# Engine programs in a block with a closing barrier, or straight in the main body: a decode kernel on one core

## The chip, the cores and the metric

The kernel runs on one core of a Trainium2 chip. Its traces show five engines with instruction streams of their own, side by side: PE (matmul, busy for 63% of the span of the kernel before), DVE (vector, 64%), ACT (scalar, 14%), POOL (GpSimd, 5%) and SP (sync, which here issues every transfer in the trace's list of DMA issues, from the 4096 KB loads to the 4 KB store). The metric is the device time of one execution in microseconds (us).

The **span** is the length of the trace, from the first to the last instruction of the kernel's own program. The **time** is what counts; it is longer than the span. Their difference is called the **remainder** below. Every timed run lists both, the span to 0.1 us, so a mean of several runs gives the remainder to about 0.05 us. No trace shows where the timed execution begins: a constant part of the remainder, the same for all kernels here, may lie before the span. "The end of the timed execution" below is counted as if it began with the span; differences between kernels do not depend on that, absolute sizes do.

## The reference, cut to what matters

```python
def reference(A_x, A_k_cache, A_v_cache, A_wq, A_wo, B_x, B_W_gate, B_W_up, B_W_down, gate_w):
    ...                                               # the helpers are cut
    x = A_x
    g = _sigmoid((x * gate_w).sum(-1, keepdims=True))
    a = _A_ref(x, A_k_cache, A_v_cache, A_wq, A_wo)   # one query, window of 4096 keys, 32 heads on 8 KV heads
    b = _B_ref(x, B_W_gate, B_W_up, B_W_down)         # gated feed-forward part
    return g * a + (1 - g) * b                        # 4 x 1 x 512, bf16
```

It reads 81 MB of caches and weights and writes 4 KB.

## The kernel before

Each engine has a function that emits its program. The functions are first run without emission, which numbers the semaphore events, and then with it, inside a block:

```python
def bass_gated_mix__...(nc, A_x, ..., out):
    ...
        R = _alloc(nc, ctx)
        progs = _program(nc, plan, R, aps)
        for _, prog in progs:
            prog(None)
        for name in plan.unit:
            plan.sems[name] = ctx.enter_context(nc.semaphore(name))
        plan.emit, plan.n = True, {}
        with nc.Block() as block:
            for name, prog in progs:
                getattr(block, name)(prog)
```

What the block makes of it, as the built program shows: the main body holds the start barrier of all engines (which is there without the block too) and, for each engine, a branch to that engine's own body. Each body ends in a branch to a common closing body. There each engine drains, reports to POOL (the gathering), and waits until POOL releases them all.

The last useful work is the store of the output. SP issues it and waits for it; its wait rides on SP's branch out.

```python
    def sync(e):
        ...
        load(("OUT",), "d_out", out.rearrange("b o d -> (b o) d"), osum[:, :], waits=[("OSUM", 0), ("OSUM", 1)])
        E.wait([("OUT",)])

    def gpsimd(e):        # only the constants; POOL's program is done at 12 us
        ...
        for g in range(8):
            v = R["fold"][:, g % 4, :, :]
            aff(v, v, [[1, 4], [-1, 64]], -64 * g, ne, 1.0, ("FOLD", g), mult=4)
```

## Time and profile before

| | before |
|---|---|
| time, median of 3 runs (range) | 197.35 us (197.25 to 197.66) |
| span of the profiled run, its time | 195.3 us, 197.06 us |
| DMA | 81.01 MB read, 415 GB/s over the span |
| busiest engine | DVE, 64% |

The page of the kernel before: the span, the busy time of each engine (in us, as a share of the span, and its number of instructions), and a row of its table of forty equal slices of the span. A digit of this row is the busy share of the 16 DMA engines in tenths, and 9 means 90% or more.

```profile
span 195.3 us, 1747 instructions
...
PE 122.6 (63%) x723; PEld 51.1 (26%) x723; DVE 124.4 (64%) x153; ACT 27.5 (14%) x34; POOL 9.5 (5%) x25
...
DMA  6999999999999999999999999999999999998991
```

The DMA engines are busy for 90% or more of all but three slices, and no other engine is near that over the span: loads bound the kernel, and what a change that leaves the loads alone can still win lies before the first load and after the last one. So the two ends matter. The start, in the timeline of the kernel before (start in us, duration, engine, line, operation; in brackets the engine's idle time before it and what ended it):

```profile
0.80 1.28 ACT L598 ACT_TABLE_LOAD   x1 [0.80 <-PEq L645]
0.80 0.20 POOL L300 MEMSET ones<- 128x128 f32 x1 [0.29 <-POOLq L645]
0.80 0.39 SPq L257 DMA_DIRECT2D slots<-in_A_wq_dram  x1
...
1.35 1.98 DVE L487 MEMSET qblk<- 128x2304 uint32 x1 [1.35 <-PEq L645]
```

Line 645 is where the start barrier is made. SP issues the first load at 0.80 us. The end, in the same timeline:

```profile
193.16 0.37 ACT L624 ACTIVATE osum<-bank 4x256 bf16<-4x256 f32 x1 [8.03 <-PE bank L321]
193.19 0.42 DVE L578 CAST osum<-bank 4x256 bf16<-4x256 f32 x1 [4.29 <-PE bank L321]
193.70 0.27 SPq L257 DMA_DIRECT2D out_dram<-osum  x1
```

The timeline ends with the issue of the store at 193.70 us. The branches, drains and semaphore instructions that follow are not counted as work, but asking for the line of the block (98) shows them (count, duration in ns, then the start of the first and of the last in us; the letter q marks the engine's sequencer):

```profile
L98 POOLq EVENT_SEMAPHORE  x2: 17/17/17, 195.2 to 195.2; - x2
L98 POOLq DRAIN  x1: 497/497/497, 11.6 to 11.6; - x1
L98 PEldq DRAIN  x1: 410/410/410, 192.8 to 192.8; - x1
...
L98 SPq COMPARE_BRANCH  x1: 33/33/33, 195.0 to 195.0; - x1
L98 SPq DRAIN  x1: 7/7/7, 195.1 to 195.1; - x1
L98 SPq EVENT_SEMAPHORE  x1: 17/17/17, 195.3 to 195.3; - x1
...
L98 PEldq EVENT_SEMAPHORE  x1: 51/51/51, 195.3 to 195.3; - x1
```

The unrounded records give the order: the output landed at 194.942 us, SP's waiting branch was recorded at 194.958, SP's drain at 195.122, POOL's two instructions (gathering and release) at 195.154 and 195.232, and PE woke last, from 195.286 to 195.337. From the landing to the end of the span it is 0.395 us. Note POOL: its program was done and drained at 12 us, and it then stood in the closing barrier until 195.25.

### The profile page before, as it was taken

Reading aid. Unit: us, or ns where it says so; the run is one execution under the profiler, and the core shown is the slowest. Engines: PE = TensorE matmul, PEld = TensorE weight load, DVE = VectorE, ACT = ScalarE, POOL = GpSimd, SP = SyncE. Lnnn points to the kernel's source line nnn. Section 1 sums busy time; section 2 is a strip of 40 time slices with the busy share of each in tenths; the row PEclk is TensorE's granted clock in tenths of the full one; section 3 lists DMA queues with packets and bytes.
Section 4 is the critical chain, followed back from the end, with each engine's and each line's share of the span. In section 5 each row is a group of like instructions: output and inputs, shape, how many; then the busy total and the mean of one; then the engine's idle time right before and its main releaser. Section 6 shows DMA issues by size and latency. Waiting matters only on the chain.

```text
span 195.3 us, 1747 instructions
## 1 busy us (share of the span) xinstructions
PE 122.6 (63%) x723; PEld 51.1 (26%) x723; DVE 124.4 (64%) x153; ACT 27.5 (14%) x34; POOL 9.5 (5%) x25
## 2 busy tenths in 40 slices
PE   0209267573974797389338646865599338754975
PEld 0004122121421242133114312421133112322562
DVE  6103688999489829981998199819971997280010
ACT  2213100040031004001300130014001400420100
POOL 7830000000000000000000000000000000000000
PEclk9999859997899579969999978998769996995799
DMA  6999999999999999999999999999999999998991
GB/s 221 429 424 436 429 429 443 429 426 436 429 443 443 431 436 433 429 436 436 436 436 429 419 436 429 436 429 429 429 429 426 429 388 426 475 429 379 418 406 70
DMA packets 4046, 81.10 MB, mean 415 GB/s; under 512 B 576, under 2 KB 840, under 8 KB 1096
## 3 DMA queue, kind: packets, MB, share of 16 engines
q1 hardware_dynamic: 4040, 81.01, 97.1%
q8 instruction: 5, 0.08, 0.2%
q14 instruction: 1, 0.01, 0.0%
HBM read 81.01 MB, written 0.00 MB: 415 GB/s over the span
## 4 chain that ended last, share of the span: by engine, by line
DMA 53%; DVE 30%; PE 9%; issue 5%; SPq 1%; ACT 0%
DMA slots<-in_A_k_cache_dram 37%; DVE kt L492 21%; DMA slots<-in_A_wo_dram 9%; PE bank L321 8%; DMA gwT<-in_gate_w_dram 6%; DVE sc L528 5%; DVE qblk L518 1%; PE bank L325 1%; SPq L257 1%; DVE pT L543 1%; DVE rd L532 1%; DVE negmax L538 0%; ACT gwB L601 0%; DVE osum L578 0%; DVE mx L528 0%
## 5 line engine op out<-in xcount | busy, mean ns | idle before, releaser
L321 PE MATMUL bank<-kt,qblk 128*128 128x512 bf16 x256 | 72.6, 434 | 30.9 <-DVE kt L492 30.8
L492 DVE STREAM_TRANSPOSE kt<-slots 128x2048 f32<-128x2048 f32 x32 | 73.7, 2305 | 25.1 <-DMA slots<-in_A_k_cache_dram 25.1
L321 PEld LDWEIGHTS bank<-kt,qblk 128*128 128x128 bf16 x256 | 24.8, 106 | 73.3 <-DVE kt L492 40.1
L321 PE MATMUL bank<-slots,pT 128*64 128x512 bf16 x256 | 33.1, 417 | 4.8 <-DMA slots<-in_A_v_cache_dram 4.8
L528 DVE CUSTOM_DVE_ANT_0 sc<-bank,maskf 128x512 bf16<-128x512 f32 x32 | 21.1, 661 | 6.6 <-PE bank L321 6.6
L620 ACT ACTIVATE pe<-sc,negmax 128x2048 bf16<-128x2048 bf16 x8 | 16.0, 2002 | 58.1 <-DVE negmax L538 58.1
L321 PEld LDWEIGHTS bank<-slots,pT 128*64 128x64 bf16 x256 | 15.4, 121 | 23.1 <-issue 13.6
L543 DVE STREAM_TRANSPOSE pT<-pe 128x2048 bf16<-128x2048 bf16 x8 | 18.5, 2312 | 2.2 <-ACT pe L620 2.2
L605 ACT ACTIVATE osb<-bank 128x512 bf16<-128x512 f32 x8 | 4.8, 597 | 84.2 <-PE bank L321 84.2
L321 PE MATMUL bank<-rd,grpb 128*128 128x32 bf16 x8 | 1.5, 192 | 18.9 <-DVE rd L532 18.9
L556 DVE TENSOR_TENSOR oq<-bank,recip 64x128 bf16<-64x128 f32 x2 | 0.9, 434 | 12.3 <-PE bank L321 12.2
L321 PEld LDWEIGHTS bank<-rd,grpb 128*128 128x128 bf16 x8 | 0.8, 97 | 22.4 <-DVE rd L532 22.4
L496 DVE COPY xT<-bank 128x16 bf16<-128x16 bf16 x1 | 0.2, 166 | 8.4 <-PE bank L325 8.4
L321 PE MATMUL bank<-slots,xT 128*4 128x512 bf16 (+1 forms) x64 | 5.3, 490 | 0.0
L518 DVE TENSOR_SCALAR qblk<-bank 32x64 uint32<-32x64 uint32 x16 | 2.9, 215 | 2.9 <-PE bank L325 2.9
L321 PE MATMUL bank<-slots,oq 128*4 128x256 bf16 x64 | 4.0, 272 | 1.2 <-DVE oq L556 1.1
L321 PE MATMUL bank<-maskr,maskl 128*128 128x512 bf16 x1 | 0.6, 606 | 5.9 <-POOL maskr L297 5.9
L325 PE MATMUL bank<-identb,xsb 4*128 4x4 bf16 x4 | 0.3, 166 | 6.1 <-DMA xsb<-in_A_x_dram 6.1
L297 POOL TENSOR_SCALAR_AFFINE_SELECT fold<-fold 128x256 bf16<-128x256 bf16 x8 | 3.3, 417 | 1.1
L321 PEld LDWEIGHTS bank<-slots,oq 128*4 128x4 bf16 x64 | 2.6, 84 | 2.5 <-issue 1.3
L578 DVE CAST osum<-bank 4x256 bf16<-4x256 f32 x1 | 0.4, 418 | 4.3 <-PE bank L321 4.3
L487 DVE MEMSET qblk<- 128x2304 uint32 x1 | 2.0, 1978 | 1.4 <-PEq L645 1.4
(59 smaller groups left out, 41.4 us busy)
## 6 DMA issues: line engine op xcount, KB each, us to landing
slots<-in_A_k_cache_dram SPq DMA_DIRECT2D x8, 4096.0 KB, 25.0
slots<-in_A_v_cache_dram SPq DMA_DIRECT2D x8, 4096.0 KB, 30.0
slots<-in_A_wq_dram SPq DMA_DIRECT2D x1, 4096.0 KB, 12.5
slots<-in_A_wo_dram SPq DMA_DIRECT2D x3, 1024.0 KB, 15.5
slots<-in_B_W_gate_dram SPq DMA_DIRECT2D x1, 1792.0 KB, 19.7
slots<-in_B_W_up_dram SPq DMA_DIRECT2D x1, 1792.0 KB, 23.6
slots<-in_B_W_down_dram SPq DMA_DIRECT2D x1, 1792.0 KB, 18.6
slots<-in_A_wo_dram SPq DMA_DIRECT2D x1, 512.0 KB, 18.4
```

The lines of the kernel that those rows point to most:

```text
L257: E.op(lambda: e.dma_start(dst, src), ev=ev, waits=waits, ctr=ctr)
L297: op(lambda: e.affine_select(dst, src, pattern, cmp, fill, base=base, channel_multiplier=mult), ev)
L321: E.op(lambda: t.matmul(out_, lhsT, rhs, start=start, stop=stop, tile_position=pos, skip_group_check=True), ev=ev, waits=waits)
L325: E.op(lambda: t.transpose(out_, in_, idn), ev=ev, waits=waits)
L487: E.op(lambda: v.memset(qblk[:, :, :, :, :].rearrange("p s h c e -> p (s h c e)"), 0.0), ev=("QZ",))
L492: E.op(lambda: v.transpose(kt[:, f, :].bitcast(FP32), slot("k", s)[:, 4096 * f:4096 * f + 4096].bitcast(FP32)), ev=("E", "KT", s, f), waits=w)
L518: E.op(lambda dst=dst, r=r, g=g: v.tensor_scalar(dst, src[r, g, 0:B, :, :], 0, None, op0=ALU.bitwise_or), ev=("E",) + keys[1] if (q, g) == ...
L528: E.op(lambda: v.tensor_tensor_reduce(sc[:, 512 * f:512 * f + 512], banks[scb(key)], R["maskf"][:, :], 1.0, -3.0e38, ALU.add, ALU.max, mx4 ...
L532: E.op(lambda: v.tensor_tensor(rd32[:, :, :], bc(R["own8"][:, :].unsqueeze(2), 2, 4), bc(mx4[:, :].unsqueeze(1), 1, 8), ALU.mult), ev=("MA ...
L543: E.op(lambda: v.transpose(pT[:, s % 2, :], pe[:, :]), ev=("E", "PT", s), waits=[("EXP", s)] + ([("PV", s - 2)] if s >= 2 else []))
L605: E.op(lambda: a.activation(osb[:, s, :], ob(s), ACTF.Copy), ev=("NORM", s), waits=[("PV", s)])
L620: E.op(lambda: a.activation(pe[:, :], sc[:, :], ACTF.Exp, bias=negmax[:, s % 2:s % 2 + 1], scale=SCALE, accum_out=rowsum[:, s:s + 1]), ev= ...
```

## The change

The intent is to leave out what the block adds: a branch into each engine's body, a branch out, and the closing barrier. The whole diff:

```diff
-        with nc.Block() as block:
+        if True:
             for name, prog in progs:
-                getattr(block, name)(prog)
+                prog(getattr(nc, name))
```

The wait for the output stays and becomes an instruction of SP. In the built program, each engine's other instructions are the same in the same order.

## The prediction

> **What bounds the kernel now.** The loads do. The row of forty slices shows the DMA engines at 9 tenths in 37 of them, mean 415 GB/s over 195.3 us; no compute engine is above 64% busy (DVE). All loads leave one queue, SP. The first is issued at 0.80 us (timeline), the last weight piece lands at 192.70 (chain of waits). Then come PE 0.43, DVE's copy 0.42, the output store's issue at 193.70 (0.27 long), and SP's wait for it, 1.0 us (SP's waits). The span is 195.3 us; the time is 197.35, some 2 us more, outside the trace's span.
>
> **What the change removes.** On each engine the order of instructions is the same but for a branch at either end; the sequencers' records show more.
>
> 1. Entry: one branch per engine. In the records SP passes the start barrier at 0.720 us and issues its first load at 0.798, a gap of 78 ns for the wait and the branch. A like pair without a branch stands at the end: SP's wait at 193.637, its store at 193.702, 65 ns. [...] It is on the critical path: all loads shift with it. DVE's first memset starts late (barrier passed at 0.73, memset at 1.35), and may start up to 0.5 us earlier; worth nothing, as DVE then idles 8.4 us. The start barrier (0.60 to 0.78) stays.
>
> 2. Exit: the output has landed at about 194.96, where SP's waiting branch is recorded (33 ns). After it come a 131 ns gap, SP's drain at 195.122, Pool's gathering at 195.154, its release at 195.232, and the last engine's wake at 195.286, which ends at 195.337. All of it, 0.38 us, is after the last useful event, wholly exposed, and goes. The wait for the output stays, as an instruction of its own. The other engines' drains ran beside the store.
>
> Nothing is added; waits, tiles, transfers and their order do not move. Estimated from those durations: entry 0.03, exit 0.38, about 0.4 us.
>
> 3. What follows the span. [...] No trace shows it; I put 0.05.
>
> **Prediction.** 197.35 - 0.03 - 0.38 - 0.05 = 196.9 us, range 196.3 to 197.4 (before's three runs spread over 0.4 us). Faster by over 2%: 1.5%; within 2%: 97.5%; slower by over 2%: 1%. The span of the trace should be about 194.9 us.
>
> **What would show it right.** No drains, gathering or release at the end; the last record is SP's wait for the output; first load issued 0.01 to 0.05 us sooner after the barrier; last weight piece landing within 0.3 us of 192.7; distance from the landing of the output to the end of the span near 0 rather than 0.38.
>
> **What would make it wrong.** [...] If loads run at another rate by chance, 0.1% of 415 GB/s is already 0.2 us.

The sum is printed as it was recorded: 197.35 - 0.03 - 0.38 - 0.05 = 196.9 us. Of the 0.03 for the entry (and of the 0.01 to 0.05 in the list of signs) the two gaps of 78 and 65 ns give 0.013, and nothing measured stands behind the 0.05. After the first cut, "it" is the branch in; the chain that ended last begins with SP's first load at 0.80 us, and no run shows the loads shifted by the branch. Only the 0.38 was read whole from the trace.

## The result

| | before | after |
|---|---|---|
| time, median of 6 runs (range) | 197.26 us (197.06 to 197.66) | 196.4 us (196.18 to 196.7) |
| profiled run: time | 197.06 us | 196.18 us |
| span | 195.337 us | 194.893 us |
| first load issued | 0.798 us | 0.800 us |
| output landed | 194.942 us | 194.860 us |
| landing to the end of the span | 0.395 us | 0.033 us |
| remainder (time less span) | 1.723 us | 1.287 us |

The ratio is 0.9955, with a 95% interval of 0.9942 to 0.9969: 0.45% faster, which counts as the same at a limit of 2% but is clear of noise. A ratio is the mean time of one kernel's runs over that of the other's runs of the same rounds, so it is not quite the ratio of the medians in the table.

The page of the kernel after:

```profile
span 194.9 us, 1736 instructions
...
DMA  6999999999999999999999999999999999999992
```

The DMA row is as full as before. The start and the end in the timeline of the kernel after:

```profile
0.80 0.40 SPq L257 DMA_DIRECT2D slots<-in_A_wq_dram  x1
...
1.35 1.98 DVE L487 MEMSET qblk<- 128x2304 uint32 x1 [1.35 <-PEq L645]
...
193.08 0.37 ACT L624 ACTIVATE osum<-bank 4x256 bf16<-4x256 f32 x1 [7.69 <-PE bank L321]
193.11 0.42 DVE L578 CAST osum<-bank 4x256 bf16<-4x256 f32 x1 [3.96 <-PE bank L321]
193.62 0.27 SPq L257 DMA_DIRECT2D out_dram<-osum  x1
```

The first load and DVE's first memset start when they did before. At the end nothing is left on line 98; SP's two waits there are now both on line 70, the helper that emits waits:

```profile
L70 SPq EVENT_SEMAPHORE  x2: 17/17/17, 193.6 to 194.9; - x2
```

SP's waits, first of the kernel before, then of the kernel after (what SP waited for: us in total, number of times, longest):

```profile
SPq L98 <- DMA out_dram<-osum: 1.0, 1, 1.0
...
SPq L98 <- PEq L98: 0.2, 1, 0.2
```

```profile
SPq L70 <- DVE osum L578: 7.2, 1, 7.2
SPq L70 <- DMA out_dram<-osum: 1.0, 1, 1.0
```

The wait for the store is the same 1.0 us; the wait in the barrier (0.2 us, put down to PE) is gone.

So of the 0.88 us between the two profiled runs, 0.08 is an earlier landing of the output, 0.36 came from the end of the span, and **0.44 is not in the trace at all**: the remainder fell from 1.723 to 1.287. The six timed runs of the kernel after confirm it: remainders of 1.22 to 1.30 us, mean 1.26. The experiments ask where that half came from.

### The profile page after: what moved, and what is told of

The parts are those of the page before. It is cut to its first block, busy times and chain, and to the rows that moved or that the text cites. A ratio compares the mean times of both kernels' runs of the same rounds, so it can differ in the third digit from the quotient of the medians.

```text
span 194.9 us, 1736 instructions
## 1 busy us (share of the span) xinstructions
PE 123.4 (63%) x723; PEld 51.9 (27%) x723; DVE 124.4 (64%) x153; ACT 27.5 (14%) x34; POOL 9.6 (5%) x25
## 4 chain that ended last, share of the span: by engine, by line
DMA 46%; DVE 25%; PE 21%; issue 6%; SPq 0%; ACT 0%
DMA slots<-in_A_k_cache_dram 25%; PE bank L321 19%; DVE kt L492 18%; DMA slots<-in_A_v_cache_dram 15%; DMA gwT<-in_gate_w_dram 6%; DVE sc L528 4%; PE bank L325 2%; DVE qblk L518 1%; DVE oq L556 0%; DVE rd L532 0%; DVE negmax L538 0%; SPq L257 0%; ACT gwB L601 0%; DVE osum L578 0%; DVE mx L528 0%
## 5 line engine op out<-in xcount | busy, mean ns | idle before, releaser
L321 PE MATMUL bank<-slots,pT 128*64 128x512 bf16 x256 | 33.6, 422 | 5.7 <-DMA slots<-in_A_v_cache_dram 5.7
```

Of the source, the lines that this page charges most:

```text
L321: E.op(lambda: t.matmul(out_, lhsT, rhs, start=start, stop=stop, tile_position=pos, skip_group_check=True), ev=ev, waits=waits)
```

## The experiments

Three theories of the remainder:

- **A, arrival.** Something follows each engine's own program that takes a certain time from that engine's end (called its **share** below); no trace here shows it. Without a barrier, the shares of four engines pass while SP waits for the output; with one, all start late together.
- **B, branches.** The branches and the separate closing body cost it, wherever the engines stand.
- **C, chance.** The remainder varies from run to run.

Every kernel of this section gave a correct result. All were timed over five rounds, beside runs of the kernel before on the same chip; e1 to e4 shared one chip, the three of e5 another and the four of e6 a third. "Landing to end" is from the landing of the output to the end of the timed execution, in the profiled run: 2.12 us before, 1.32 after.

### e1: the closing barrier alone

```diff
             for name, prog in progs:
                 prog(getattr(nc, name))
+        nc.all_engine_barrier()
```

> The remainder (a run's time less its span) was 1.72 us in the profiled run of the kernel before and 1.2 to 1.3 us in all runs of the kernel after. The main body of the kernel after, with only the closing barrier of all engines put back and no branch. Theory A (the four other engines do their share of what follows the kernel while SP waits for the output, unless a barrier holds them): span up by 0.4 to about 195.3 us, remainder up to 1.7, time about 197.2, so ratio 1.00 to the kernel before. Theory B (the branches and the separate closing body cost it, wherever the engines stand): span 195.3, remainder 1.25, time about 196.8, ratio 0.998. Theory C (the extra 0.4 us is chance): remainder anywhere from 1.2 to 1.7 from run to run.

Measured: 197.06 us, ratio 0.9992 (0.9978 to 1.0006), so all of the gain is lost again. Mean remainder 1.75 us (five runs, 1.73 to 1.76). The kernel before on this chip, nine runs: 1.73 (1.70 to 1.80). From the line of the barrier:

```profile
L101 POOLq EVENT_SEMAPHORE  x2: 17/17/17, 195.2 to 195.2; - x2
L101 POOLq DRAIN  x1: 497/497/497, 11.6 to 11.6; - x1
...
L101 SPq DRAIN  x1: 13/13/13, 195.1 to 195.1; - x1
```

The barrier does it without any branch, as theory A has it. C falls too, as the two groups of remainders do not overlap. The span ended 0.294 us after the landing, against 0.395 before, so the branch out was worth 0.10 us of the exit: SP's drain is recorded 0.056 us after the start of its wait here, and 0.164 us after the start of its waiting branch before.

### e2: no barrier, but all engines late

```diff
+        for name in ("tensor", "vector", "scalar", "gpsimd"):
+            getattr(nc, name).wait_ge(plan.sems["d_out"], 16)
```

> The kernel after, with all five engines waiting for the output at their ends; no barrier, no branch, no drain. Theory A: span as after, about 195.0 us, but remainder 1.7, time about 196.8. Theory B: span 195.0, remainder 1.25, time about 196.4 as the kernel after.

Measured: 197.14 us, ratio 0.999 (0.9977 to 1.0002). The end of the program is five waits that finish within 0.05 us of each other (SP's own stands on line 70; the other four):

```profile
L102 ACTq EVENT_SEMAPHORE  x1: 17/17/17, 195.2 to 195.2; - x1
L102 POOLq EVENT_SEMAPHORE  x1: 17/17/17, 195.2 to 195.2; - x1
L102 DVEq EVENT_SEMAPHORE  x1: 21/21/21, 195.2 to 195.2; - x1
L102 PEldq EVENT_SEMAPHORE  x1: 51/51/51, 195.2 to 195.2; - x1
```

The span ends 0.080 us after the landing, so there is hardly any exit in it; but the mean remainder is 1.76 us, and landing to end is 1.83. Nothing differs from the kernel after but four added waits, of 17 to 51 ns, that hold the other engines until the output has landed. This is the cleanest test, and A passes it. (The landing itself was 0.3 us later than in the profiled run of after, as the store was issued that much later, at 193.93 against 193.62 us; so the expected time of 196.8 was missed by 0.3, but the remainder does not contain that.)

### e3: the branches without the barrier

```diff
-        if True:
+        with nc.Block() as block:
             for name, prog in progs:
-                prog(getattr(nc, name))
+                getattr(block, name)(prog)
+        end = nc.cur_bb.bb
+        ...
+        end.instructions = []
```

> The block with its branches in and out as in the kernel before, but with the closing barrier's instructions (drains, gathering, release) taken out. Theory A: like the kernel after, span about 195.0 us plus at most 0.15 for SP's branch, remainder 1.25, time 196.4 to 196.6. Theory B: remainder 1.7, time about 196.8. Entry: first load issued at 0.80 us in both theories, since the trace of after already shows that the entry branch cost nothing.

Measured: 196.53 us, ratio 0.9961 (0.9949 to 0.9974), mean remainder 1.33 us, landing to end 1.38. Of line 98 only SP's branch is left:

```profile
L98 SPq COMPARE_BRANCH  x1: 33/33/33, 195.1 to 195.1; - x1
```

The branches in and out together cost some 0.1 us (196.53 against 196.4), and by the mean remainder 0.07 (1.33 against 1.26). B falls. The first load went out at 0.798 us, as in every kernel here with or without a branch before it (0.790 to 0.800).

### e4 and e5: one engine last

SP's wait for the output is taken out and put at the end of one other engine:

```diff
+        nc.scalar.wait_ge(plan.sems["d_out"], 16)      # e4; nc.tensor, nc.vector, nc.gpsimd in e5
 ...
-        E.wait([("OUT",)])                             # in SP's program
```

> The kernel after, with the wait for the output moved from SP to ACT, so SP ends once it has issued the store and ACT ends last. Theory A: span 195.0 us; the remainder is that of ACT's own share after the kernel, and differs from 1.25 if the engines' shares differ (my guess 1.0 to 1.6). Theory B: remainder 1.25, time 196.4.

> The kernel after with the wait for the output moved from SP to PE, so PE alone ends last. From the landing of the output to the end of the timed execution it took 2.12 us before, 1.32 after (SP last), 1.44 with ACT last, 1.83 with all five last. Max rule (each engine has a fixed share of work after its end, all run side by side, and the longest sets the time): one of PE, DVE and POOL alone must give about 1.83, and I expect PE to be it: 1.83 for PE, time about 196.9. Serial rule (the five shares run one after the other, and come to 1.83 only if all are late): PE alone 1.3 to 1.5, time about 196.5.

> DVE alone ends last. Max rule: between 1.3 and 1.83 us from the landing to the end; if PE is the long one, about 1.4 to 1.5 as for ACT. Serial rule: 1.3 to 1.5.

> POOL alone ends last. Max rule: between 1.3 and 1.83 us from the landing to the end; about 1.4 to 1.5 if PE is the long one. Serial rule: 1.3 to 1.5. If POOL is below 1.3, a kernel with POOL last beats the kernel after.

| last engine | time, median | ratio to before | its end to the end of the execution | landing to end |
|---|---|---|---|---|
| SP (after) | 196.4 | 0.9955 | 1.29 us | 1.32 us |
| DVE | 196.45 | 0.9968 | 1.39 us | 1.44 us |
| ACT | 196.47 | 0.9962 | 1.40 us | 1.44 us |
| PE | 196.66 | 0.9973 | 1.53 us | 1.61 us |
| POOL | 197.11 | 1.000 | 1.79 us | 1.83 us |
| all five (e2) | 197.14 | 0.999 | | 1.83 us |

The mean remainders of all runs agree: SP 1.26, DVE 1.38, ACT 1.41, PE 1.51, POOL 1.80 us. Runs of one kernel differ by up to 0.11 us, so DVE and ACT cannot be told apart; the other steps are clear, though the kernels ran on different chips. The absolute sizes hold only if the timed execution begins with the span; a constant part before it would be contained in all five alike.

The expectation named the wrong engine: PE was to be the long one and is only the second. It is POOL. With POOL alone late, landing to end is 1.83 us, exactly that of all five late, so the shares run side by side and the longest one counts; serial shares would have given each engine alone less. In the kernel with POOL last, the only instruction after the store is one 17 ns wait:

```profile
L101 POOLq EVENT_SEMAPHORE  x1: 17/17/17, 194.9 to 194.9; - x1
```

and it takes the whole gain away. SP, which the kernel after happens to leave last, is the cheapest of the five.

### e6: the rule put to a test

From these singles follows a rule: the execution ends at the latest of each engine's own end plus its share (POOL 1.79, PE 1.53, ACT 1.40, DVE 1.39, SP 1.29 us). Four more kernels on one chip:

```diff
+        for name in ("tensor", "vector", "scalar"):                                  # e6_all_but_pool
+            getattr(nc, name).wait_ge(plan.sems["d_out"], 16)
```

```diff
+        nc.gpsimd.wait_ge(plan.sems["dve"], plan.ev[("OSUM", 1)][1])                 # e6_pool_late_1024
+        nc.gpsimd.memset(R["fold"][:, :, :, :], 0.0)
```

```diff
+        nc.gpsimd.wait_ge(plan.sems["dve"], plan.ev[("OSUM", 1)][1])                 # e6_pool_late_512
+        nc.gpsimd.memset(R["maskr"][:, :], 0.0)
```

> As the run in which all five engines waited for the output, but POOL left free to end at 12 us. The singles give each engine's share from its own end to the end of the timed execution: POOL 1.79 us, PE 1.53, ACT 1.40, DVE 1.39, SP 1.29. Max rule: PE is now the longest, so the remainder falls from 1.76 to 1.5 (landing to end 1.61 instead of 1.83), time about 196.7. Rival, serial rule (the shares add when the engines are late together): the remainder stays near 1.7 as four of five are still late, time about 196.9.

> The kernel after, with SP last as there, and POOL made late by a useless memset of 128x1024 bf16 that starts when DVE has written the output (about 193.6 us; such a memset took 0.95 us at the start of the kernel), so POOL ends about 0.2 to 0.3 us before the output lands. Max rule: the end is the later of POOL's end plus 1.79 and SP's end plus 1.29, so POOL sets it: landing to end about 1.55 us instead of 1.32, remainder about 1.5, time about 196.65. Rival (POOL costs only when it ends last): 1.32, remainder 1.27, time 196.4.

> The same with a memset of 128x512 (0.52 us at the start of the kernel), so POOL ends about 0.6 to 0.7 us before the output lands, which is more than the 0.5 by which its share is longer than SP's. Max rule: hidden, landing to end 1.32, remainder 1.27, time 196.4. If the remainder is above 1.35, the rule is wrong.

> The kernel after with one comment line more, as a measure on this chip beside the others: remainder 1.26, time about 196.4, ratio 0.9955 to the kernel before.

In the run with all but POOL late, the added waits are those of ACT, DVE and PE alone (PEldq is PE's sequencer):

```profile
L102 ACTq EVENT_SEMAPHORE  x1: 17/17/17, 195.5 to 195.5; - x1
L102 DVEq EVENT_SEMAPHORE  x1: 21/21/21, 195.5 to 195.5; - x1
L102 PEldq EVENT_SEMAPHORE  x1: 51/51/51, 195.5 to 195.5; - x1
```

| kernel | time, median | ratio to before | mean remainder | landing to end |
|---|---|---|---|---|
| all but POOL late | 196.69 | 0.9971 | 1.54 us | 1.59 us |
| POOL late, 1024 | 196.6 | 0.9964 | 1.42 us | 1.47 us |
| POOL late, 512 | 196.32 | 0.995 | 1.27 us | 1.29 us |
| the kernel after again | 196.41 | 0.9954 | 1.25 us | 1.28 us |
| the kernel before on this chip | 197.33 | 1 | 1.73 us | |

The two useless memsets, in the timelines of the long and of the short one:

```profile
193.90 0.95 POOL L102 MEMSET fold<- 128x1024 bf16 x1 [181.86 <-DVE osum L580]
193.93 0.27 SPq L259 DMA_DIRECT2D out_dram<-osum  x1
```

```profile
193.71 0.52 POOL L102 MEMSET maskr<- 128x512 bf16 x1 [181.66 <-DVE osum L580]
193.74 0.27 SPq L259 DMA_DIRECT2D out_dram<-osum  x1
```

Neither memset touches the critical path: the output landed at 195.164 and 194.982 us, after POOL's ends at 194.850 and 194.232. Yet the long one costs 0.17 us of remainder beside the kernel after on the same chip, and the short one nothing that can be told from its scatter (1.27 against 1.25). That is what separates "late" from "last": POOL need not end last to be the engine that counts. By the rule it is in time if it ends 0.50 us (1.79 less 1.29) before SP; the two runs lie on either side, at 0.35 us (too late) and 0.78 us (in time), so the limit is bracketed, not measured.

Worked out by the rule from the engines' ends in each trace, against the time of the same profiled run:

| kernel | engine that counts, its end + its share | rule | measured |
|---|---|---|---|
| before | POOL 195.249 + 1.79 | 197.04 | 197.06 |
| closing barrier alone | POOL 195.249 + 1.79 | 197.04 | 197.06 |
| all late | POOL 195.212 + 1.79 | 197.00 | 197.00 |
| branches only | SP 195.120 + 1.29 | 196.41 | 196.45 |
| all but POOL late | PE 195.528 + 1.53 | 197.06 | 197.04 |
| POOL late, 1024 | POOL 194.850 + 1.79 | 196.64 | 196.63 |
| POOL late, 512 | SP 195.015 + 1.29 | 196.30 | 196.27 |
| after again | SP 195.307 + 1.29 | 196.60 | 196.55 |

None of these eight runs served to find the shares, and the rule meets all within 0.05 us. The first four were known when the rule was written down, though, and the last repeats the kernel after, so three are true forecasts of it. One expectation missed its size: the remainder of the long memset was to be about 1.5 and was 1.42, because POOL ended 0.31 us before the landing, not 0.2 to 0.3; with the true end the rule gives the measured time. No kernel beats the kernel after: the short memset's 196.32 lies within its spread.

## Why the prediction was right or wrong

**The bound and the slices: right.** The loads bound both kernels, and the DMA row is unchanged.

**Entry, 0.03 us: nothing.** The first load went out at 0.798 us before and 0.800 after. The prediction had compared the 78 ns from SP's start barrier to its first load with 65 ns of a wait and a store elsewhere, and put the difference down to the branch; the rest of its 0.03 us was an estimate that no trace showed. The kernel after, without the branch, has the same gap (0.721 to 0.800, 79 ns), so the two pairs were not alike. The traces record no entry branch and show no cost of one: the first instructions after the start barrier started within 2 ns of the same time with the branch and without it (SP 0.798 and 0.800 us, ACT 0.797 in both, POOL 0.798 in both, DVE 1.351 in both). What SP's 0.10 us at the exit consists of is not shown. DVE's late first memset, which the prediction held might be the branch's doing, started at 1.35 us in both.

**Exit inside the span, 0.38 us: right, measured 0.36.** Landing to the end of the span fell from 0.395 to 0.033 us, as SP's wait still takes an instruction (17 ns, from 194.876). Of the exit, 0.10 us was the branch out and the rest the barrier (e1). The other engines' drains cost nothing there: the last of them, DVE's, ended at 193.663 us, before the store was issued at 193.702. The span came out at the predicted 194.9, with 0.08 us of it from an earlier landing.

**After the span, 0.05 us: the term that was mis-sized; it measured 0.44** (0.47 by the mean remainders, 1.73 and 1.26)**.** The prediction's 0.05 was the author's guess, with no measure of the engines' shares behind it. What counts is SP's share (1.29, the shortest) against POOL's (1.79, the longest). The block's barrier held POOL, idle since 12 us, until 195.25 us, and so put the longest share behind the last event of all. Freed at 12 us, POOL's share is hidden whole (all but POOL late: landing to end 1.59 us, against 1.83 with POOL too).

**The sum.** 0.03 + 0.38 + 0.05 = 0.46 us were predicted; the profiled pair gives 0.00 + 0.36 + 0.44, and 0.08 by the landing, together 0.88. The time of 196.4 us lies in the stated range, near its low end, and "within 2%" was right. That it lies there is owed to the width of the range, which was set from a scatter of 0.4 us, and not to the sum: the gain was nearly double the forecast. "Within 2%" would have been right without any gain.

**What was to make it wrong** did not happen: the loads ran at nearly the same rate (415 GB/s over the span before, 416 after), and the output landed 0.08 us earlier. Nor did the barrier's cost turn up again after the span: the remainder fell, by 0.44 us.

**What stays open.** What an engine's share consists of, and why POOL's is the longest: no trace covers it. Every timed run lists a span and so was recorded; no run shows whether the shares are the same without recording.

## What to carry to other kernels

Leave each engine's program as soon as its work is done, and let one engine alone wait for the output: here a closing barrier cost not only its own steps (0.36 us with its branch out, 0.26 without: 0.294 in e1 less 0.033) but also what follows the programs of engines that had been idle for long, which it lined up behind the last store (0.44 us). All kernels here stayed correct without the barrier; each kernel has to be checked for that. If there is a choice of the engine that ends last, SP was the cheapest here and POOL the dearest, by 0.5 us. Read the remainder, time less span, beside the span: half of this change was in no trace.
